# Three chained layers on one core: weight tiles shared by two batches, an attention with more buffers, another place for the decoding

## The chip, the cores and the metric

The kernel runs on one core of one Trainium2 chip. The metric is the device time of one execution in microseconds (us). The kernel before takes 1176.02 us, the median of three runs (1173.72 to 1176.10).

## The reference

Three layers follow each other, for 4 batches (B) of 448 positions (S) and 768 features (12 heads of 64):

```python
scores = scale * np.matmul(q, k.transpose(0, 1, 3, 2))      # causal mask, softmax over the last axis
x = softmax(scores) @ v                                     # B, S, 768
h = x.transpose(0, 2, 1) @ U @ V                            # low rank: 448 -> 32 -> 448 along S
u = x + h.transpose(0, 2, 1)
x = u + np.maximum(u @ w_ch1, 0.0) @ w_ch2                  # 768 -> 3072 -> 768
logits = x @ w_gate                                         # 4 experts, the best 2 of each position
out = sum(w[e] * (softmax_causal(x @ wq[e], x @ wk[e]) @ (x @ wv[e])) @ wo[e] for e in chosen)
```

Inputs and weights arrive as 64-bit floats.

## The kernel before, in words

**Numbers.** Matrix products run in float16 with each operand cut into a high and a low half, and three of the four products of halves are added (`PASS`), so that a product of a 128x128 weight block with 448 columns is three matmuls of 128x448. The 64-bit weights are *decoded* on the core: VectorE makes a float32 from the two words (`decode`, one TENSOR_SCALAR and two SCALAR_TENSOR_TENSOR of 128x768), ScalarE squares it for a norm, TensorE adds the norm up over the partitions (a 128x1 matmul), ScalarE scales and casts the high half, GpSimd subtracts it for the low half. `weight_tile` does this for one of 48 tiles of the MLP (the 768-3072-768 layer), stores the result to HBM (`W16`), and on a later use loads the tile from there in place of decoding it. The raw tile lands in one of two buffers (`RAW`).

**Stages.** The MLP has 4 groups of 12 tiles: 6 tiles of the first matrix and 6 of the second. A *product* is what one tile does for one batch: 18 matmuls of 128x448. `mlp(g, b)` is group g for batch b: 6 products into the hidden buffer `HID` (one buffer), 6 products added to the batch's float32 state `X3`. So a batch has 48 products, the kernel 192. `attention(b)` is the first layer of batch b with the low-rank step behind it, as 6 *pairs* of heads, counted through: batch 0 has pairs 0 to 5, batch 1 pairs 6 to 11, and so on. For each pair `softmax` makes scores on TensorE, masks and scales them on VectorE, takes exponentials on ScalarE (four per head, 112x112 to 112x448), casts the high halves of P by `HIGH` (two of four on ScalarE, two on VectorE), subtracts on GpSimd for the low halves, and transposes both by DMA; `weighted` multiplies with V, `lowrank` does the step behind. `split_u` then cuts the batch's u into halves for the MLP, which can not start before. `experts(b)` is the last layer of batch b.

**Order.** The program is recorded first, in the order of the string `ORDER`: attention of batch 0 (a0), of batch 1 (a1), MLP of batch 0 (m00 to m03), experts of batch 0 (e0), a2, the MLP of batch 1, e1, a3, the MLP of batch 2, e2, the MLP of batch 3, e3. Then `Program.issue` plans it: it walks all five engines with costs per instruction (`cost`), and of what is ready takes the smallest key. Attention has keys that rise by 4500 per half pair (`HT`), MLP products have a large one (`FILL`), so they fill what is left; decoding has the keys of `first_key`. The result is one fixed order of instructions for each engine, and on the chip each engine runs its own in order. Where the plan has TensorE idle before `WARM_END`, it puts in dummy matmuls (line 953). All planned instructions are issued at line 250, so the rows below are told apart by shape.

**Memory.** Weight tiles live in a ring of `NW` = 19 slots. `SLOTS` gives batch 0's attention more buffers for P than the others (5 instead of 3, and 4 instead of 2 for its halves), since the buffers of batch 1 are idle then. `BANKS` says which of 8 PSUM banks a stage uses; MLP products of batch 0 use two of them ("f").

Of the kernel before, what the change touches and what calls it, by code (L numbers as in the profile page):

```python
# [21 lines left out]
C = 112  # L22
NC = S // C
KD = D // 128
NG = 4
# [5 lines left out]
HIGH = ("act", "act", "dve", "dve")  # L31
# [11 lines left out]
WARM_START, WARM_END, WARM_GAP = 3000.0, 130000.0, 100.0  # L43
NW = 19
# [3 lines left out]
ORDER = "a0 a1 m00 m01 m02 m03 e0 a2 m10 m11 m12 m13 e1 a3 m20 m21 m22 m23 e2 m30 m31 m32 m33 e3"  # L48
# [4 lines left out]
class Program:  # L53
# [7 lines left out]
    def __init__(self):  # L61
        self.ops = []
        self.key = 0.0
        self.group_op = None
        self.state = {}
        self.near = {}
        self.pitch = {}
        self.idle = None

# [54 lines left out]
    def cost(self, name, method, outs, ins, kw):  # L124
        o = outs[0]
        n = 1
        for c in o.shape[1:]:
            n *= c
        if name == "pe":
            f = 4.0 if ins[0].dtype == F32 else 1.0  # L130
            c = f * max(n / 2.4 + 2.5, 36.0)
            self.work = c * (ins[0].shape[0] / 128.0) * (o.shape[0] / 128.0)

            return c * (0.62 if HD in (o.shape[0], ins[0].shape[0]) and n >= C else 1.0)
        ptr = sum(x.free_size() == 1 and n > 1 for x in ins)
        psum = any(a.space == bass.MemoryType.PSUM for a in outs + ins)
        if name == "act" and method == "dma_start":
            return 300.0
        if name == "act":
            src = 51.0 if ins[0].space == bass.MemoryType.PSUM else 94.0  # L140
            return src + n / 1.2 + 93.0 * (ptr + len(outs) - 1)
        if name == "dve":
            m = 1
            for c in ins[0].shape[1:] if ins else o.shape[1:]:
                m *= c
            m = max(m, n)
            fast = not psum and method in ("tensor_scalar", "tensor_copy", "memset")
            two = not psum and n > 32 and (fast or sum(x.free_size() > 1 for x in ins) > 1)
            return ((64.0 + (m / 2 if fast else m)) / 0.96 + 64.0 * ptr) * (1.2 if two else 1.0)
        if name == "pool":  # L150
            if method == "partition_all_reduce":
                return 374.0
            return 148.0 + 1.89 * n if method == "tensor_tensor" else 260.0 + 2.5 * n
        return 350.0 + outs[0].nbytes() / 292.0 if method == "dma_start_transpose" else 650.0

    def add(self, name, method, fn, a, k):
        outs, ins = [], []
        for key, x in list(enumerate(a)) + list(k.items()):
            if hasattr(x, "ap"):
                (outs if key in (0, "out", "accum_out") else ins).append(x)  # L160
        self.work = 0.0
        cost = self.cost(name, method, outs, ins, k)
        data = 0.0
        if method.startswith("dma"):
            nbytes = max(x.nbytes() for x in outs + ins)
            data = nbytes / (185.0 if method == "dma_start_transpose" else 360.0)
        deps = set()
        i = len(self.ops)
        if self.group_op:
            i -= 1  # L170
        for x in ins:
            r = self.region(x)
            if r is not None:
                for q in self.touching(r):
                    deps.update(self.state[q][0])
                self.state[r][1].append(i)
        for x in outs:
            r = self.region(x)
            if r is not None:
                for q in self.touching(r):  # L180
                    w, rd = self.state[q]
                    deps.update(w)
                    deps.update(rd)
                    if q[1] >= r[1] and q[2] <= r[2] and q[3] >= r[3] and q[4] <= r[4]:
                        w[:] = [i]
                        rd[:] = []
        deps.discard(i)
        if self.group_op:
            op = self.ops[-1]
            op["calls"].append((fn, a, k))  # L190
            op["cost"] += cost
            op["work"] += self.work
            op["deps"] |= deps
        else:
            op = dict(eng=name, cost=cost, data=data, deps=deps, calls=[(fn, a, k)], key=self.key,
                      work=self.work)
            self.ops.append(op)
            if self.group_op is False:
                self.group_op = True

    def issue(self):
# [9 lines left out]
        bus = 0.0  # L211
# [7 lines left out]
        while done < len(ops):  # L219
# [33 lines left out]
            if n == "pe":  # L253
# [4 lines left out]
                if not warm:  # L258
                    cost *= 2.0
            end = t + cost  # L260
# [15 lines left out]
def kernel(  # L276
# [44 lines left out]
    BANKS = {"s": (0, 1), "o": (2,), "l": (3, 4), "m": (5, 6, 7), "f": (5, 6), "r": (7,), "x": (5, 6), "y": (2, 7), "b": (3, 4)}  # L321
# [16 lines left out]
    HID = view("hid", 0, 128, F16, GF * 2 * S).rearrange("p (f l s) -> p f l s", f=GF, l=2)  # L338
# [10 lines left out]
    def hslot(r, o):  # L349
        return view(r, o, C, F16, 2 * NBLK * 128)  # L350

    SLOTS = [
        (P32[0:3] + [pslot("x3", 10752), pslot("x3", 10752 + 4480)], PHL[0:2] + [hslot("uh", 5376), hslot("ul", 5376)]),
        (P32[0:3], PHL[0:2]), (P32[0:3], PHL[0:2]), (P32[0:3], PHL[0:2]),
# [130 lines left out]
    def softmax(terms, nes, pts, last=False, kind="s", first=False):  # L485

        ps, hs = P32[0:3], PHL[0:2]
        if last:
            ps, hs = P32, PHL
        elif first:  # L490
            ps, hs = SLOTS[0]
# [28 lines left out]
        for j in range(2):  # L520
# [14 lines left out]
            sp.dma_start_transpose(out=PT[pts[j]], in_=h16[j])  # L535
# [26 lines left out]
    def weighted(vs, pts, y, dst, coef=None, kind="o"):  # L562
        shares(y, coef)
        t = psum(kind)
        with prog.group():
            for i, (lp, lv_) in enumerate(PASS):
                for j in range(NC):
                    for h, (va, pt) in enumerate(zip(vs, pts)):
# [4 lines left out]
                           PT[pt][0:C, k:k + kc * (NC - 1 - j) + 1:kc],  # L573
# [37 lines left out]
    def attention(b):  # L611
# [6 lines left out]
        for p in range(NP):  # L618
# [6 lines left out]
            if p == NP - 1 and b + 1 < B:  # L625
                v_scale(b + 1)
            i = n % 2
            prog.key = HT * 2 * n
            softmax([[(QK[i][64 * j:64 * j + 64, 1], QK[i][64 * j:64 * j + 64, 0])] for j in range(2)], -0.125,
                    [(2 * n + j) % 3 for j in range(2)], first=b == 0)  # L630
            prog.key = HT * (2 * n + 1)
            weighted([VH[:, 2 * i + j] for j in range(2)], [(2 * n + j) % 3 for j in range(2)], X3[b][:, p], XHL[i])
# [19 lines left out]
    kept = [False]  # L652
# [78 lines left out]
    def mlp(g, b):  # L731
        if b == 0:
            factors(g)
        ut = (UH[b], UL[b])
        for f in range(GF):
            early = g + b + f == 0
            t = psum("m" if kept[0] else "f")
            wt = [a.rearrange("p (k m) -> p k m", k=KD) for a in tiles[2 * GF * g + f]]
            prog.key = FILL - early
            product(t[:, 0:S], [(wt[lw][:, k], ut[lx][:, k]) for k in range(KD) for lw, lx in PASS])  # L740
            prog.key = URGENT
            act.activation(t[:, 0:S], t[:, 0:S], AF.Relu, scale=(RF if b else RF0)[:, g * GF + f:g * GF + f + 1])
            act.activation(HID[:, f, 0], t[:, 0:S], AF.Copy)
            dve.tensor_tensor(out=HID[:, f, 1], in0=t[:, 0:S], in1=HID[:, f, 0], op=ALU.subtract)
        cf, ct = CF[g % 2], CTS[g % 2]
        dve.tensor_scalar(ct, PRS[:, g:g + 1], 2.0 ** 54 / HCAP, PU[:, b:b + 1], op0=ALU.mult, op1=ALU.mult)
        dve.tensor_scalar(cf, PW2[:, g * GF:g * GF + KD], 2.0 ** 83, ct, op0=ALU.mult, op1=ALU.mult)
        for d in range(KD):
            t = psum("m" if kept[0] else "f")
            wt = [a.rearrange("p (k m) -> p k m", k=GF) for a in tiles[2 * GF * g + GF + d]]  # L750
            prog.key = FILL
            product(t[:, 0:S], [(wt[lw][:, f], HID[:, f, lx]) for f in range(GF) for lw, lx in PASS])
            prog.key = URGENT
            dve.scalar_tensor_tensor(out=X3[b][:, d], in0=t[:, 0:S], scalar=cf[:, d:d + 1], in1=X3[b][:, d],
                                     op0=ALU.mult, op1=ALU.add)
            if g == NG - 1:
                absmax(AMX[:, b * KD + d:b * KD + d + 1], X3[b][:, d])

    def experts(b):
# [3 lines left out]
        free = 3072 * next(i for i in range(NW - 5) if not held & set(range(i, i + 6)))  # L763
        if last:
            qo, vo, yo, xo = ("hid", 0), ("ring", free), ("hid", 7168), ("ring", free + 4096)
# [6 lines left out]
        if last:  # L772
            OST = [view("ring", free + 6144 + i * 1792, 128, F32, S) for i in range(6)]
        else:
            OST = [view("rd", 14848 + i * 1792, 128, F32, S) for i in range(2)]
        pts = (0, 1, 2, 3) if last else (0, 1, 0, 1)
# [126 lines left out]
    zero_pads(SLOTS[0][1])  # L903
# [25 lines left out]
    def first_key(i):  # L929
        return HT * (1 + 0.9 * i if i < 2 * GF else 12 + (i - 2 * GF) / 3)  # L930

    def group(b, g):
        for i in range(2 * GF * g, 2 * GF * (g + 1)):
            prog.key = URGENT if b else first_key(i)
            weight_tile(i, not b)
        mlp(g, b)
# [13 lines left out]
    for step in ORDER.split():  # L950
        kind, b = step[0], [int(c) for c in step[1:]]
        {"a": attention, "m": group, "e": moe}[kind](*b)
# [47 lines left out]
```

## Time and profile before

| | |
|---|---|
| median of three runs | 1176.02 us |
| the profiled execution | 1177.93 us |
| its span, first to last instruction | 1176.2 us |
| TensorE busy | 1088.9 us (93%), 392 dummy matmuls in it |
| VectorE busy | 678.1 us (58%) |
| ScalarE busy | 546.7 us (46%) |
| GpSimd busy | 371.3 us (32%) |
| DMA | 162 loads and 54 stores of 384 KB tiles, 48 of 768 KB raw tiles, 88 transposes |
| granted TensorE clock, mean | 0.967 of full speed |

A share over the whole span says little here, since the stages have different limits. The profile is read by stretches: 0 to 150 us (attention of batch 0, with decoding), 150 to 391.4 us (attention of batch 1, the rest of the decoding, MLP of batch 0), 391.4 to 975 us (MLP of batches 1 and 2, attention of batches 2 and 3, experts of batches 0 and 1), 975 to the end (the rest of batch 3).

### The profile page before, as it was taken

How to read it: one execution, taken by the hardware profiler on the slowest of the kernel's cores; microseconds unless marked ns; L12 is line 12 of the kernel's file. 1: busy time of each engine (PE TensorE's matmuls, PEld its weight loads, DVE VectorE, ACT ScalarE, POOL GpSimd, SP SyncE). 2: the span in 40 equal slices, each digit the busy share in tenths (PEclk: the TensorE clock that was granted, in tenths of full speed). 3: DMA queues.
4: the chain of work that ended last, by engine and by line, in shares of the span. 5: the costliest groups of instructions: out<-in, count | busy, mean ns of one | idle time of the engine just before them, and what ended most of it. 6: DMA issues, size and time to landing. Idle time of an engine off the chain costs nothing.

```text
span 1176.2 us, 18782 instructions
## 1 busy us (share of the span) xinstructions
PE 1088.9 (93%) x6888; PEld 571.7 (49%) x6888; DVE 678.1 (58%) x1831; ACT 546.7 (46%) x1317; POOL 371.3 (32%) x419
## 2 busy tenths in 40 slices
PE   7899969979988999999999999999999997899895
PEld 3454434434444455445555554455555544355452
DVE  8869888998889765665432555654224333111453
ACT  4755767676577544575412456652122323121142
POOL 3755755766453102454200034540000012000012
PEclk9999978998999999999999999999999998999998
DMA  7887888897786754998734349984443255331023
GB/s 195 208 195 245 211 199 242 260 229 206 230 265 222 239 189 112 213 231 200 175 108 120 96 107 216 234 180 118 122 121 108 82 131 112 125 121 54 1 40 87
DMA packets 220141, 192.57 MB, mean 164 GB/s; under 512 B 176304, under 2 KB 179504, under 8 KB 220048
## 3 DMA queue, kind: packets, MB, share of 16 engines
q1 hardware_dynamic: 220048, 191.36, 61.0%
q8 instruction: 54, 0.88, 0.3%
q14 instruction: 39, 0.32, 0.1%
HBM read 121.60 MB, written 26.74 MB: 126 GB/s over the span
## 4 chain that ended last, share of the span: by engine, by line
PE 65%; DVE 9%; issue 3%; ACT 3%; DMA 2%; POOL 2%; POOLq 0%; SPq 0%; DVEq 0%; ACTq 0%
PE bank L250 65%; DVE arena L250 9%; ACT arena L250 2%; POOL arena L250 2%; DMA arena<-in_v_dram 1%; DMA arena<-in_w_dram 0%; DMA arena<-in_we_dram 0%; DMA arena<-w 0%; ACT bank L250 0%; POOLq L995 0%; SPq L250 0%; DVEq L250 0%; ACTq L250 0%; POOLq L250 0%
## 5 line engine op out<-in xcount | busy, mean ns | idle before, releaser
L250 PE MATMUL bank<-arena 128*128 128x448 f16 (+12 forms) x6496 | 1006.5, 332 | 70.0 <-DVE arena L250 40.8
L250 PEld LDWEIGHTS <-arena 128*128 128x128 f16 (+4 forms) x5960 | 489.2, 106 | 489.8 <-issue 124.9
L250 POOL TENSOR_TENSOR arena<-arena 112x336 f16<-112x336 f32 (+6 forms) x408 | 369.1, 924 | 796.2 <-ACT arena L250 719.6
L250 ACT ACTIVATE arena<-arena 128x768 f16<-128x768 f32 (+10 forms) x671 | 376.6, 591 | 282.8 <-DVE arena L250 267.6
L250 DVE TENSOR_TENSOR arena<-bank,arena 128x448 f16<-128x448 f32 (+2 forms) x160 | 95.4, 600 | 215.2 <-ACT arena L250 183.4
L250 DVE CUSTOM_DVE_ANT_0 arena<-bank,arena 112x112 f32<-112x112 f32 (+4 forms) x280 | 125.7, 475 | 62.6 <-PE bank L250 55.1
L250 ACT ACTIVATE bank<-bank,arena 128x448 f32<-128x448 f32 x96 | 57.8, 603 | 222.8 <-PE bank L250 221.8
L250 DVE SCALAR_TENSOR_TENSOR arena<-bank,arena 128x448 f32<-128x448 f32 (+1 forms) x120 | 73.4, 614 | 148.0 <-PE bank L250 125.0
L250 DVE SCALAR_TENSOR_TENSOR arena<-arena 128x768 int32<-128x768 int32 (+5 forms) x159 | 154.9, 993 | 5.3 <-ACT arena L250 4.2
L250 ACT ACTIVATE arena<-bank 128x448 f16<-128x448 f32 (+2 forms) x160 | 82.6, 523 | 74.7 <-PE bank L250 72.8
L250 DVE TENSOR_SCALAR arena<-arena 128x1 f32<-128x1 f32 (+9 forms) x367 | 90.7, 267 | 20.1 <-ACT arena L250 9.7
L953 PE MATMUL bank<-arena 128*128 128x448 f16 x392 | 89.8, 376 | 13.4 <-DVE arena L250 12.4
L250 DVE CAST arena<-arena 112x336 f16<-112x336 f32 (+2 forms) x160 | 85.4, 547 | 2.1 <-PE bank L250 1.0
L250 PEld LDWEIGHTS bank<-arena 64*112 64x112 f32 (+5 forms) x536 | 49.4, 176 | 55.9 <-issue 18.9
L953 PEld LDWEIGHTS <-arena 128*128 128x128 f16 x392 | 39.1, 105 | 54.3 <-issue 25.9
L250 DVE TENSOR_REDUCE arena<-arena 128x1 f32<-128x448 f32 (+7 forms) x107 | 58.2, 546 | 9.5 <-DMA arena<-in_v_dram 5.2
L250 ACT ACTIVATION_READ_ACCUMULATOR arena<-arena 112x1 f32 (+1 forms) x304 | 57.0, 188 | 0.0
L250 ACT ACTIVATE arena<-bank,arena 64x128 f16<-64x128 f32 (+3 forms) x85 | 34.2, 405 | 44.6 <-PE bank L250 38.7
L250 DVE TENSOR_TENSOR arena<-arena 112x8 f16<-112x8 f32 (+4 forms) x69 | 24.6, 368 | 1.4
L250 DVE DVE_READ_ACCUMULATOR2_ANT arena<- 112x1 f32 (+1 forms) x280 | 22.7, 81 | 0.0
L250 DVE TENSOR_SCALAR arena<-bank 128x1 f32<-128x1 f32 x48 | 7.2, 149 | 12.8 <-PE bank L250 12.7
L250 DVE RECIPROCAL arena<-arena 112x8 f32<-112x8 f32 (+1 forms) x36 | 7.0, 195 | 0.7
(12 smaller groups left out, 13.6 us busy)
## 6 DMA issues: line engine op xcount, KB each, us to landing
arena<-w SPq DMA_DIRECT2D x162, 384.0 KB, 3.3
arena<-in_w_dram SPq DMA_DIRECT2D x48, 768.0 KB, 5.6
w<-arena SPq DMA_DIRECT2D x54, 384.0 KB, 3.1
arena<-in_qk_dram SPq DMA_DIRECT2D x24, 448.0 KB, 5.6
arena<-in_v_dram SPq DMA_DIRECT2D x24, 224.0 KB, 5.0
out_dram<-arena SPq DMA_DIRECT2D x24, 224.0 KB, 2.6
arena<-in_we_dram SPq DMA_DIRECT2D x6, 384.0 KB, 4.6
arena<-arena SPq DMA_TRANSPOSE x88, 4.6
```

Of the source, the lines that this page charges most:

```text
L250: fn(*a, **k)
L953: prog.idle = lambda: nc.tensor.matmul(bank[:, 7, 64:512], ZERO.to_broadcast([128, 128]), ZERO.to_broadcast([128, S]), start=True, stop=True)
```

## The change

- `ORDER` becomes "a0 a1 m00 m01 m101 m20 m30 e0 a2 m21 m31 e1 a3 m02 m12 m22 m32 e2 m03 m13 m23 m33 e3". The first digit is now the group, the rest are the batches: m101 is group 1 for batches 0 and 1. Both attentions come first, then group 0 for batch 0 and for batch 1 with the same 12 tiles, group 1 for both in turn, tile by tile, then groups 2 and 3 for batch 0, its experts, and so on. `group` loads or decodes tiles only where the group differs from the last one; 24 of the 144 reloads go.
- `first_key` moves the decoding back: the 12 tiles of group 0 are spread over both attentions, the other 36 have keys behind them.
- `HIGH`: all high halves of P on ScalarE.
- `SLOTS`: the second attention has 5 and 4 buffers too.
- The hidden buffer is doubled, and the ring has 15 slots for it. MLP products use four PSUM banks ("g") between the second attention and the first expert stage.
- The planner's costs: VectorE and GpSimd instructions that use the port they share are planned one after the other, transposes are planned as faster, dummies go on to 210000 of the planner's units.

```diff
-HIGH = ("act", "act", "dve", "dve")
+HIGH = ("act", "act", "act", "act")
...
-WARM_START, WARM_END, WARM_GAP = 3000.0, 130000.0, 100.0
-NW = 19
+WARM_START, WARM_END, WARM_GAP = 3000.0, 210000.0, 100.0
+NW = 15
...
-            two = not psum and n > 32 and (fast or sum(x.free_size() > 1 for x in ins) > 1)
-            return ((64.0 + (m / 2 if fast else m)) / 0.96 + 64.0 * ptr) * (1.2 if two else 1.0)
+            self.port = not psum and n > 1 and (fast or sum(x.free_size() > 1 for x in ins) > 1)
+            return (64.0 + (m / 2 if fast else m)) / 0.96 + 64.0 * ptr + 80.0 * (self.port and n > 32)
...
+            if o["port"]:
+                t = max(t, port)
+                port = t + cost
...
-        ("ring", NW * 3072), ("rd", RD), ("hid", GF * 2 * S * 2),
+        ("ring", NW * 3072), ("rd", RD), ("hid", 2 * GF * 2 * S * 2),
...
+    SPARE = [hslot("uh", 5376), hslot("ul", 5376)]
     SLOTS = [
-        (P32[0:3] + [pslot("x3", 10752), pslot("x3", 10752 + 4480)], PHL[0:2] + [hslot("uh", 5376), hslot("ul", 5376)]),
-        (P32[0:3], PHL[0:2]), (P32[0:3], PHL[0:2]), (P32[0:3], PHL[0:2]),
+        (P32[0:3] + [pslot("x3", 10752), pslot("x3", 10752 + 4480)], PHL[0:2] + SPARE, PT[0:3]),
+        (P32[0:3] + [pslot("hid", 10752), pslot("hid", 10752 + 4480)], PHL[0:2] + SPARE, PT[0:3]),
+        (P32[0:3], PHL[0:2], PT[0:3]), (P32[0:3], PHL[0:2], PT[0:3]),
     ]
...
-    def mlp(g, b):
-        if b == 0:
+    def mlp(g, bs):
+        if 0 in bs:
             factors(g)
-        ut = (UH[b], UL[b])
+        bank = "m" if kept[0] else "g" if started[0] else "f"
         for f in range(GF):
...
+            for b in bs:
+                early = g + b + f == 0
+                t = psum(bank)
+                wt = [a.rearrange("p (k m) -> p k m", k=KD) for a in tiles[2 * GF * g + f]]
...
     def first_key(i):
-        return HT * (1 + 0.9 * i if i < 2 * GF else 12 + (i - 2 * GF) / 3)
+        return HT * (1 + 2.6 * i if i < 2 * GF else 32 + (i - 2 * GF) / 3)
...
+    def group(g, bs):
+        if last_group[0] != g:
+            for i in range(2 * GF * g, 2 * GF * (g + 1)):
+                prog.key = URGENT if g in made else first_key(i)
+                weight_tile(i, g not in made)
+            made.add(g)
+            last_group[0] = g
+        mlp(g, bs)
```

How the change moves instructions, at two places. The first is VectorE at the decoding of tile 27 (of 48). Before, this stands in the middle of pair 10's softmax: 128x768 are the decoding, "ISA" rows of 112 partitions the masking of scores, 128x448 evictions of MLP products, 128x1 the small steps of a norm.

```order
L250 TENSOR_SCALAR arena<-arena 128x768
L250 SCALAR_TENSOR_TENSOR arena<-arena 128x768
L250 TENSOR_SCALAR arena<-bank 128x1
L250 ISA arena<-bank,arena 112x448
L250 ISA arena 112x1
L250 TENSOR_SCALAR arena<-arena 128x1
L250 SCALAR_TENSOR_TENSOR arena<-arena 128x768
L250 TENSOR_SCALAR arena<-arena 128x1
L250 ISA arena<-bank,arena 112x448
L250 ISA arena 112x1
L250 TENSOR_TENSOR arena<-bank,arena 128x448
L250 TENSOR_SCALAR arena<-arena 128x1
```

In the changed kernel the same decoding stands in the MLP of group 1:

```order
L252 TENSOR_SCALAR arena<-arena 128x768
L252 TENSOR_SCALAR arena<-bank 128x1
L252 TENSOR_TENSOR arena<-bank,arena 128x448
L252 TENSOR_SCALAR arena<-arena 128x1
L252 SCALAR_TENSOR_TENSOR arena<-arena 128x768
L252 TENSOR_SCALAR arena<-arena 128x1
L252 SCALAR_TENSOR_TENSOR arena<-arena 128x768
L252 TENSOR_SCALAR arena<-arena 128x1
L252 TENSOR_TENSOR arena<-bank,arena 128x448
```

No softmax stands there any more: for one decoded tile there are two evictions, one of each batch. On TensorE the norms of tiles 0 to 9 stand before the last scores of the second attention and those of tiles 10 to 14 before the first product of batch 1; before, all 48 stand ahead of batch 1's first.

The second place is the SP queue, which issues all DMAs, at the load of pair 4's q and k (in_qk). Before, it stands behind the transposes (128x20x112) of pair 3:

```order
L250 DMA_TRANSPOSE arena<-arena 128x20x112
L250 DMA_TRANSPOSE arena<-arena 128x8x128
L250 DMA_TRANSPOSE arena<-arena 128x20x112
L250 DMA arena<-in_v_dram 112x512
L250 DMA arena<-in_w_dram 128x768 x2
L250 DMA arena<-in_qk_dram 128x896
L250 DMA arena<-in_v_dram 112x512
```

In the changed kernel it stands between the two transposes of pair 1:

```order
L252 DMA_TRANSPOSE arena<-arena 128x20x112
L252 DMA_TRANSPOSE arena<-arena 128x8x128
L252 DMA arena<-in_qk_dram 128x896
L252 DMA arena<-in_w_dram 128x768
L252 DMA_TRANSPOSE arena<-arena 128x20x112
L252 DMA w<-arena 128x1536
L252 DMA arena<-in_v_dram 112x512
```

The loads of a pair have moved ahead by two pairs of transposes.

## Rows read from the trace of the kernel before

**Rows 1.** Busy time: stretch, us, PE, PEld, DVE, ACT, POOL (instructions), PEclk, DMA share, GB/s

```profile
0.00:150.00 150.00, 131.35 (x854) 66.09 (x855) 125.04 (x369) 93.50 (x239) 91.44 (x102) 0.96 0.79 208
150.00:391.40 241.40, 202.88 (x1242) 105.66 (x1242) 210.71 (x504) 165.62 (x335) 130.70 (x124) 0.92 0.83 235
391.40:975.00 583.60, 582.32 (x3806) 308.98 (x3807) 281.76 (x812) 241.19 (x633) 128.32 (x167) 1.00 0.59 153
975.00:1176.20 201.20, 172.33 (x988) 90.99 (x988) 60.60 (x148) 46.38 (x112) 20.80 (x27) 0.92 0.28 75
```

**Rows 2.** The same of line 953 (dummy matmuls) alone: PE, PEld

```profile
0.00:150.00 150.00, 87.19 (x386) 38.34 (x387) 0.96 0.79 208
150.00:391.40 241.40, 2.60 (x6) 0.73 (x5) 0.92 0.83 235
```

**Rows 3.** Chain that ended last: start us, us, what

```profile
391.40 159.20 PE bank L250 x1096
...
983.64 10.51 issue
...
1003.09 4.17 DMA arena<-w
```

**Rows 4.** Groups by shape, TensorE, to 391.4 us, then from there: busy, mean ns

```profile
L250 PE MATMUL bank<-arena 128*128 128x448 f16 x756 | 161.8, 364 | 18.3 <-DVE arena L250 16.4 <-ACT arena L250 1.6
...
L250 PE MATMUL bank<-arena 128*128 128x448 f16 x3132 | 623.0, 356 | 12.0 <-DVE arena L250 3.9 <-DMA arena<-w 3.0 <-ACT arena L250 2.8
```

**Rows 5.** Busy time, 1025 to 1050 us

```profile
1025.00:1050.00 25.00, 25.00 (x134) 12.92 (x132) 3.91 (x7) 5.44 (x10) 0.00 (x0) 1.00 0.40 124
```

**Rows 6.** Groups by shape, ScalarE, 7.5 to 126.6 us

```profile
L250 ACT ACTIVATE arena<-arena 128x768 f16<-128x768 f32 x21 | 18.5, 880 | 13.1 <-DVE arena L250 12.9
L250 ACT ACTIVATE arena<-arena 112x448 f32<-112x448 f32 x12 | 7.9, 657 | 0.0
```

**Rows 7.** The same, 470 to 559 us

```profile
L250 ACT ACTIVATE arena<-arena 112x448 f32<-112x448 f32 x12 | 7.9, 659 | 2.3 <-DVE arena L250 2.3
```

**Rows 8.** Busy time, 470 to 559 us

```profile
470.00:559.00 89.00, 88.93 (x662) 44.90 (x661) 54.80 (x183) 53.67 (x161) 43.61 (x58) 1.00 0.91 215
```

**Rows 9.** Timeline of ScalarE: start us, us, instruction

```profile
590.51 2.89 ACT L250 ACTIVATE arena<-arena 128x448 f16<-128x448 f32 x5
```

**Rows 10.** Groups by shape, whole span: busy us, mean ns, idle before

```profile
L250 DVE SCALAR_TENSOR_TENSOR arena<-arena 128x768 int32<-128x768 int32 x96 | 109.2, 1139 | 0.6
L250 DVE TENSOR_TENSOR arena<-bank,arena 128x448 f16<-128x448 f32 x112 | 69.0, 621 | 165.0 <-ACT arena L250 164.4
L250 DVE CAST arena<-arena 112x448 f16<-112x448 f32 x64 | 42.4, 663 | 0.5 <-ACT arena L250 0.5
L250 DVE TENSOR_SCALAR arena<-arena 128x768 int32<-128x768 int32 x48 | 35.0, 730 | 7.4 <-DMA arena<-in_w_dram 3.7 <-POOL arena L250 3.2 <-issue 0.2
L250 DVE CAST arena<-arena 112x336 f16<-112x336 f32 x64 | 31.7, 506 | 0.1
L250 ACT ACTIVATE arena<-arena 112x224 f16<-112x224 f32 x64 | 23.5, 376 | 0.2
```

**Rows 11.** Timeline of VectorE, then of GpSimd

```profile
51.46 2.06 DVE L250 CAST arena<-arena 112x336 f16<-112x336 f32 x1
...
49.84 4.92 POOL L250 TENSOR_TENSOR arena<-arena 112x224 f16<-112x224 f32 x4
```

**Rows 12.** Timeline of the SP queue (DMA issues), 73 to 85 us

```profile
73.39 9.72 SPq L250 DMA_TRANSPOSE arena<-arena  x3
...
84.97 0.43 SPq L250 DMA_DIRECT2D arena<-in_qk_dram  x1
```

**Rows 13.** SP queue, raw weight loads of tiles 34 and 47

```profile
301.80 0.37 SPq L250 DMA_DIRECT2D arena<-in_w_dram  x1
...
372.00 0.33 SPq L250 DMA_DIRECT2D arena<-in_w_dram  x1
```

**Rows 14.** Groups by shape, TensorE, 423 to 593.4 us

```profile
L250 PE MATMUL bank<-arena 128*128 128x448 f16 x612 | 124.5, 353 | 0.0
```

More of the change, by code (lines that the diff above doesn't have):

```diff
@@ L483, in scaled_copy, with softmax @@
             dve.tensor_scalar(o, a, scale, None, op0=ALU.mult)
-    def softmax(terms, nes, pts, last=False, kind="s", first=False):
+    def softmax(terms, nes, pts, last=False, kind="s", slots=None):
         ps, hs = P32[0:3], PHL[0:2]
@@ L489, in softmax @@
             ps, hs = P32, PHL
-        elif first:
-            ps, hs = SLOTS[0]
+        elif slots:
+            ps, hs = slots
         k = heads[0]
@@ L762, in experts @@
         held = {(ring_n[0] - 1 - i) % NW for i in range(NE)}
-        free = 3072 * next(i for i in range(NW - 5) if not held & set(range(i, i + 6)))
+        two = 3072 * next(i for i in range(NW - 1) if not held & {i, i + 1})
         if last:
-            qo, vo, yo, xo = ("hid", 0), ("ring", free), ("hid", 7168), ("ring", free + 4096)
+            qo, vo, yo, xo = ("hid", 0), ("ring", two), ("hid", 7168), ("ring", two + 4096)
         else:
@@ L772, in experts @@
         if last:
-            OST = [view("ring", free + 6144 + i * 1792, 128, F32, S) for i in range(6)]
+            OST = [view("hid", 10752 + i * 1792, 128, F32, S) for i in range(6)]
         else:
             OST = [view("rd", 14848 + i * 1792, 128, F32, S) for i in range(2)]
-        pts = (0, 1, 2, 3) if last else (0, 1, 0, 1)
+        pts = PT if last else PT[0:2] * 2
         ks, ko, kl = "xyy" if last else "sll" if b == B - 2 else "sol"
@@ L929, in first_key @@
     def first_key(i):
-        return HT * (1 + 0.9 * i if i < 2 * GF else 12 + (i - 2 * GF) / 3)
[L932 to L936, printed above, removed]
+        return HT * (1 + 2.6 * i if i < 2 * GF else 32 + (i - 2 * GF) / 3)
+    made = set()
+    last_group = [None]
+    def group(g, bs):
[6 more added lines that the diff above has]
+        mlp(g, bs)
     def moe(b):
@@ L950 @@
     for step in ORDER.split():
-        kind, b = step[0], [int(c) for c in step[1:]]
-        {"a": attention, "m": group, "e": moe}[kind](*b)
+        kind, bs = step[0], [int(c) for c in step[1:]]
+        if kind == "a":
+            attention(*bs)
+            started[0] = bs[0] == 1
+        elif kind == "e":
+            moe(*bs)
+            last_group[0] = None
+        else:
+            group(bs[0], bs[1:])
     prog.idle = lambda: nc.tensor.matmul(bank[:, 7, 64:512], ZERO.to_broadcast([128, 128]), ZERO.to_broadcast([128, S]), start=True, stop=True)
```

77 lines of the change are left out of this document (42 added, 35 removed).

## The prediction

> **What bounds the kernel now.** I read the busy time by stretch first [rows 1], then the chain that ended last [rows 3], then the groups by shape. From 391.4 to 975 us TensorE is busy 582.3 of 583.6 us at full clock: here only matmuls count. Ahead of that it isn't TensorE: up to 391.4 us it is busy 334.2 us, and 89.8 of these are dummies [rows 2]. VectorE is busy 125.0 of the first 150 us and 210.7 of the next 241.4, the fullest engine of both. So the kernel has two parts, one that VectorE and the waits around it set, and one that TensorE sets. The chain says the same: from 391.4 us it runs on TensorE for 159 us at a stretch, and leaves it for long only near 983 and 1003 us [rows 3].
>
> How much is done in the first part? The 128x448 matmuls are 756 up to 391.4 us [rows 4], or 42 products of 18: batch 0's MLP but for its last six. Behind stand 3132: 150 products (2700) and 432 of the four expert stages. At peak 134 of them take 25.0 us [rows 5], 0.1866 us each, 3.36 us a product.
>
> **The change, as a sum.** I call S the time at which batch 1's first product starts in the changed kernel. By the order of instructions only batch 0's group 0 (12 products) is done by then, so 180 products are left where at 391.4 us 150 were left. The rest is the same work. So the span is S + (1176.2 - 391.4) + 30 x 3.36 = S + 784.8 + 100.7 = S + 885.5, plus what the new second part loses. Below S = 290.7 the change gains.
>
> *S.* In the first attention, 7.5 to 126.6 us holds 12 exponentials of 112x448, two a pair, so 6 pairs at 19.85 us each; 21 casts or squares of 128x768, two a tile, say that 10.5 tiles were decoded there, 1.75 a pair [rows 6]. The third attention has no decoding beside it: 89 us for 6 pairs, 14.8 each [rows 7]. The difference, 5.0 us, is 2.9 us a decoded tile. The changed order has 10 norms ahead of the second attention's last scores, 0.83 a pair: 14.8 + 0.83 x 2.9 = 17.2 us. Before, the second attention has its 6 pairs among 30 tiles and three MLP groups; that falls away. Its larger buffers and the earlier loads are in this pace: in the SP queue three transposes held it from 73.4 to 83.1 us, and pair 4's loads came only at 84.97 [rows 12]; they now stand ahead of these.
>
> *The casts.* Per pair, two of 112x336 (0.506 us) and two of 112x448 (0.663) leave VectorE, 2.34 us [rows 10]. ScalarE gets four; it shows none of these shapes. From below they cost 0.376 us (its cast of 112x224, rows 10), from above 0.657 (its 112x448 exponential, rows 6): 1.5 to 2.6 us a pair, I take 2.1. So a pair's pace moves by something between -2.3 and +2.6 us; I take -1.2, half of what VectorE gives up, since the trace has VectorE as the fuller engine. Pace 16.0, bounds 14.9 and 19.8. A cast of 112x336 that began at 51.46 us took 2.06 us while GpSimd ran four subtractions without a pause from 49.84 to 54.76 us [rows 11]: four times its mean.
>
> The Trainium skill (SBUF — State Buffer, Who interferes with whom) says that a VectorE cast in a two-port mode and a GpSimd instruction lock each other out for a whole instruction. The row agrees; by that rule alone the casts give back their full 2.34 us and GpSimd's waits too, and the sum would be some 14 us lower.
>
> Behind the third attention's last softmax, at 559 us, come 34.4 us of weighting, low rank and splitting until its u is cut, at 593.4 us [rows 9]. S = 7.5 + 12 x 16.0 + 34.4 = 233.9. A bound from VectorE's load: 335.8 us busy up to 391.4 [rows 1], less 30 tiles of 0.730 + 2 x 1.139 = 3.0 us (90.2), less 48 casts (28.1), leaves 217.4; at the first stretch's density (125.0 of 150) that is 261 us, not counting the evictions and small steps that go too. From below: pairs at 14.8 - 2.3 = 12.5 us give 192.
>
> *The second part.* Two terms. (a) 33 tiles are now decoded between S and the norm of tile 47, and the norms stand in TensorE's stream among products it could do: 879 of the 128x448, 164.0 us, 4.97 us a tile. Before, with little else in the way, the raw loads of tiles 34 and 47 are 70.2 us apart [rows 13], 5.40 us a tile, which is 14.2 us more in all. From above: a tile now has nearly two products' evictions beside it, not one, 0.62 us more on VectorE [rows 10]: 6.02 us, 34.7 in all. From below 0, where the loads have the queue to themselves. I take 7. (b) Beside the first expert stage and the third attention, 423 to 593.4 us, TensorE did 612 of the 128x448, 108 of them the experts' own, so 504 of products [rows 14]; in the changed order 393 stand there, since batch 1 has only two groups left. If those stages need their 170 us anyway, TensorE idles 111 x 0.1866 = 20.7 us; if not, nothing. VectorE is busy 54.8 of 89 us there and ScalarE 53.7, so there is room [rows 8], though DMA's share is 0.91. I take 5.
>
> *At nothing.* The 24 reloads saved: the DMA share in the MLP is 0.40 [rows 5], so they are hidden, and were. Four fewer ring slots: in a run of products a slot's tile comes free 14 products, 47 us, before its next is wanted. Dummies: they fill idle time. The last expert attention has no cover: its two pairs' casts change it by -5 to +5 us, taken at 0. Stalls near 983 and 1003 us [rows 3], transposes and then a weight load behind them, stay: the order there has the same pieces.
>
> The Trainium skill (Perfetto Trace Analysis, Optimizing Scalar/DVE Operations) holds that an operation with a fast mode is quicker on VectorE, and that moving it pays where VectorE is saturated. It isn't from 470 us on [rows 8], so by that rule the later pairs lose a little; here a cast's mean on VectorE, 0.51 to 0.66 us, is no shorter than my estimate for ScalarE, so I add nothing. By the rule the sum would be up to 4 us higher.
>
> **Sum.** 233.9 + 885.5 + 7 + 5 = 1131.4 us of span. The profiled execution took 1.7 us more than its span and 1.9 more than the median, so span and median differ by 0.2 us: 1131.
>
> **Rivals.**
> - *Decoding sets the pace of the MLP behind it.* TensorE waits at norms, 6.02 us a tile: 1131.4 - 7 + 34.7 = 1159 us. For it: 5.40 us a tile was reached with one batch's evictions. Against: no softmax shares VectorE there now.
> - *Too little to do beside the third attention.* 1131.4 - 5 + 20.7 = 1147 us. For it: DMA at 0.91. Against: TensorE never waited there, so nothing shows that the stages need the 170 us.
> - *ScalarE becomes the engine that each pair waits for (slower than before).* It has exponentials, casts, V and decoding, and if a pair keeps the first attention's 19.85 us and the casts come on top, the pace is 21.95 us, S = 7.5 + 263.4 + 34.4 = 305.3, the span 1203 us. It decides from a pace of 19.7 us on. For it: 19.85 is what the first attention did with these buffers. Against: ScalarE was busy 93.5 of 150 us there, and decoding per pair halves.
>
> That the sharing does nothing is part of the forecast: what gains is the place of the work, not the saved loads.
>
> **Chances.** Forecast 0.56; decoding 0.19; cover 0.17; ScalarE 0.08. The likeliest's own range, with pace 14.9 to 17.5, is 1118 to 1150. For 8 in 10 I go to 1105 below (a pace of 14.9 with nothing lost behind gives 1106) and to 1165 above, past both rivals that still gain. A measurement can't tell a change under 0.2%. Faster 0.91, same 0.02, slower 0.07: only the last rival, and not all of it, ends above 1178.
>
> **What would show it.** Right: batch 1's first product near 234 us, the 12 pairs 16 us apart, then TensorE busy to near 930 us with no dummies. S wrong: ScalarE over nine tenths busy up to S, or long gaps before scores. (a) wrong: TensorE waiting for ScalarE or VectorE at 128x1 matmuls between 234 and 410 us. (b) wrong: gaps of TensorE before the cut of batch 2's u. Wrong as a whole: a pace over 19.7 us a pair, or a second part in which TensorE is under 95% busy.

## The result and the profile after

The changed kernel takes 1123.1 us (median of 4 runs, 1116.7 to 1124.5) against 1176.1: ratio 0.954, interval 0.950 to 0.958. The prediction was 1131 with a range of 1105 to 1165. The profiled execution's span is 1122.8 us.

Busy time by stretch, changed kernel: stretch, us, PE, PEld, DVE, ACT, POOL (instructions), PEclk, DMA share, GB/s.

```profile
0.00:222.30 222.30, 211.30 (x1550) 110.05 (x1551) 177.39 (x542) 175.55 (x456) 135.23 (x162) 1.00 0.87 217
222.30:434.60 212.30, 210.94 (x1155) 113.07 (x1153) 158.90 (x338) 124.81 (x200) 77.29 (x68) 1.00 0.65 216
434.60:770.00 335.40, 323.84 (x2348) 173.39 (x2347) 167.36 (x566) 201.57 (x568) 117.18 (x154) 0.99 0.69 162
770.00:952.00 182.00, 172.48 (x1004) 91.84 (x1003) 52.66 (x132) 52.17 (x119) 13.20 (x18) 0.99 0.40 116
952.00:1122.80 170.80, 152.83 (x883) 82.31 (x880) 52.15 (x127) 41.84 (x102) 13.28 (x18) 0.95 0.27 77
```

The boundary between the two parts, at 391.4 us in [rows 1], is now at 222.3 us: S, the start of batch 1's first product. In the row that ends there three resources are busy at once, and none is full: VectorE 80%, ScalarE 79%, DMA 0.87. TensorE's 211.3 us are again filled with dummies, as in [rows 2]; here are theirs alone (PE, PEld):

```profile
0.00:222.30 222.30, 96.12 (x436) 40.90 (x436) 1.00 0.87 217
```

From S on TensorE idles 1.4 + 11.6 + 9.5 + 18.0 = 40.4 us; from 391.4 us on it idled 30.2 before. Its busy time from S is 860.1 us; before it was 754.7 from 391.4, and the 30 products that move over make that 855.4. So the second part is 900.5 us: the 885.5 of the prediction, 10.2 more idle and 4.7 more busy.

The chain that ended last, changed kernel: start us, us, what.

```profile
529.04 8.21 DMA arena<-arena
...
759.83 138.68 PE bank L252 x774
...
920.64 11.07 issue
...
938.73 3.01 DMA arena<-w
```

The two late stalls of [rows 3] are both still there, as predicted. New are the transposes (a DMA from arena to arena) between 460 and 750 us, with short pieces of ScalarE and GpSimd between them; before, the chain ran on TensorE there but for some 9 us near 700.

### The profile page after: what moved, and what is told of

It is laid out like the page before. It is cut to its first block, busy times and chain, and to the rows that moved or that the text cites. A ratio compares the mean times of both kernels' runs of the same rounds, so it can differ in the third digit from the quotient of the medians.

```text
span 1122.8 us, 18857 instructions
## 1 busy us (share of the span) xinstructions
PE 1071.4 (95%) x6932; PEld 570.7 (51%) x6932; DVE 608.5 (54%) x1703; ACT 595.9 (53%) x1445; POOL 356.2 (32%) x419
## 4 chain that ended last, share of the span: by engine, by line
PE 41%; DMA 8%; ACT 4%; issue 3%; POOL 2%; DVE 1%; SPq 1%; POOLq 0%; ACTq 0%; DVEq 0%
PE bank L252 41%; DMA arena<-arena 6%; ACT arena L252 3%; POOL arena L252 2%; DVE arena L252 1%; DMA out_dram<-arena 1%; SPq L252 1%; DMA arena<-w 1%; DMA arena<-in_v_dram 0%; ACT bank L252 0%; POOLq L1029 0%; POOLq L252 0%; ACTq L252 0%; DVEq L252 0%
## 5 line engine op out<-in xcount | busy, mean ns | idle before, releaser
L252 PE MATMUL bank<-arena 128*128 128x448 f16 (+11 forms) x6496 | 985.7, 327 | 45.5 <-DMA arena<-arena 18.3
L252 POOL TENSOR_TENSOR arena<-arena 128x384 f16<-128x384 f32 (+6 forms) x408 | 354.0, 889 | 757.6 <-ACT arena L252 732.4
L252 ACT ACTIVATE arena<-arena 112x112 f32<-112x112 f32 (+13 forms) x799 | 431.9, 578 | 209.8 <-DVE arena L252 169.8
L252 DVE SCALAR_TENSOR_TENSOR arena<-arena 128x768 int32<-128x768 int32 (+6 forms) x159 | 150.7, 968 | 2.1 <-ACT arena L252 1.3
L252 DVE TENSOR_SCALAR arena<-arena 128x1 int32<-128x1 int32 (+8 forms) x367 | 84.9, 254 | 36.8 <-ACT arena L252 21.7
L987 PE MATMUL bank<-arena 128*128 128x448 f16 x436 | 96.1, 362 | 2.0 <-DVE arena L918 1.0
L252 DVE TENSOR_REDUCE arena<-arena 128x1 f32<-128x448 f32 (+6 forms) x107 | 57.8, 545 | 4.6 <-DMA arena<-in_we_dram 2.3
L252 ACT ACTIVATE arena<-bank,arena 64x128 f16<-64x128 f32 (+2 forms) x85 | 34.1, 406 | 39.2 <-PE bank L252 32.7
L252 DVE CAST arena<-arena 112x8 f16<-112x8 f32 x32 | 15.5, 486 | 3.7 <-PE bank L252 3.4
L252 DVE TENSOR_REDUCE arena<-bank 1x1 f32<-1x128 f32 (+2 forms) x14 | 3.9, 276 | 7.9 <-PE bank L252 7.9
```

The source lines that it names most:

```text
L252: fn(*a, **k)
L987: prog.idle = lambda: nc.tensor.matmul(bank[:, 7, 64:512], ZERO.to_broadcast([128, 128]), ZERO.to_broadcast([128, S]), start=True, stop=True)
```

## The experiments

"Time" is the median; the ratio is to the kernel before, with its interval; the changed kernel has 0.954. Runs of one kernel lie up to 9 us apart, so single profiles differ by some us without a reason. Differences are those of the medians; the kernel before took 1172.9 to 1176.1 us beside the several runs, so by the ratios they come out up to 5 us larger.

**Only the order and its due times undone.**

```
-ORDER = "a0 a1 m00 m01 m101 m20 m30 e0 a2 ..."   # groups for two batches
+ORDER = "a0 a1 m00 m10 m20 m30 e0 a2 m01 m11 ..."
-  1 + 2.6 * i if i < 2 * GF else 32 + (i - 2 * GF) / 3
+  1 + 0.9 * i if i < 2 * GF else 12 + (i - 2 * GF) / 3
```

(and the dummies' end in the plan at 130 us, as before)

> The changed kernel with the old order and decoding keys alone: group by group for one batch (group 0 to 3 of batch 0, then e0, a2, batch 1), decoding among both attentions, dummies to 130000. Theory (the place of the decoding and of the products makes the gain): batch 1's first product comes no sooner than 360 us, dummy-free TensorE from about 390 us, and the time goes back to 1160 to 1178 us. Rival (the attention itself became faster by casts, buffers and planning; the order is only along): the first part shortens anyway and the time stays under 1140 us.

1185.4 us, ratio 1.009 (1.007 to 1.012). That is 7 us above the theory's range, and the rival (under 1140) is excluded. The casts, the buffers and the planner's costs without the order make the kernel slower: 62 us lie between the two orders, and nothing of the gain is left in the old one. The order, the due times of the decoding and the sharing of tiles, which the old order has no place for, were undone together; only the sharing has runs of its own, further below.

```profile
0.00:270.50 270.50, 231.32 (x1566) 123.21 (x1567) 197.09 (x598) 197.46 (x488) 157.70 (x177) 0.92 0.83 209
270.50:406.50 136.00, 125.34 (x670) 66.39 (x668) 111.11 (x236) 86.69 (x137) 61.48 (x52) 0.96 0.74 247
```

Busy time as above, this kernel. The second attention ends at 270 us instead of 221, since more tiles are decoded beside it, and TensorE waits 10.7 us in the next 136. Batch 1's first relu comes at 406.5 us, so its first product starts near 403.

**The same and the casts back on VectorE.**

```
-HIGH = ("act", "act", "act", "act")
+HIGH = ("act", "act", "dve", "dve")
```

> Old order and keys and casts as before; the rest (buffers, 15 slots, two hidden buffers, four PSUM banks, planner's costs) as changed. Theory: the casts gain only where the attentions stand alone in front; with decoding among them VectorE is full of it and ScalarE too, so against e5 (1185 us) the time changes by under 8 us: 1177 to 1190 us, no faster than the kernel before. Rival A (casts on ScalarE hurt where decoding is among the attentions): 1165 to 1174 us. Rival B (the casts help everywhere by 2 us a pair): 1205 us or more.

1207.8 us, ratio 1.030 (1.028 to 1.033): the theory fell and rival B holds, the casts bring 22 us in the old order too. What is left of the change (ring of 15 slots, two hidden buffers, the planner's costs, borrowed buffers), put into the old order, costs 32 us against the kernel before. I did not take this apart further.

**Only the casts back**, by the same line, in the new order.

> The changed kernel with two of four casts back on VectorE. Theory: the first part grows by 0.5 to 1.2 us a pair (6 to 14 us), and of the 11.4 us in which TensorE idles beside the third and fourth attention most goes, since the casts on ScalarE lengthen each pair there: 1118 to 1130 us, batch 1's first product at 228 to 236 us. Rival A (the casts make the gain): over 1140 us. Rival B (the idle time there comes from transposes planned as faster, not from the casts): the idle time stays at 8 us or more, and the time is 1129 to 1137 us.

1155.0 us, ratio 0.983 (0.980 to 0.986): rival A. 32 us are lost, 27 of them before S. ScalarE's timeline shows where: the first exponential, the last pair's first one of 112x448 and batch 1's first relu in this kernel, then the last two in the changed one, whose first exponential is at 17.68.

```profile
17.79 0.39 ACT L252 ACTIVATE arena<-arena 112x112 f32<-112x112 f32 x1 [15.71 <-DVE arena L252]
...
203.27 0.67 ACT L252 ACTIVATE arena<-arena 112x448 f32<-112x448 f32 x1 [1.08 <-DVE arena L252]
...
252.83 1.18 ACT L252 ACTIVATE bank<-bank,arena 128x448 f32<-128x448 f32 x2 [0.94 <-PE bank L252]
```

```profile
176.01 0.67 ACT L252 ACTIVATE arena<-arena 112x448 f32<-112x448 f32 x1 [0.50 <-DVE arena L252]
...
225.75 0.61 ACT L252 ACTIVATE bank<-bank,arena 128x448 f32<-128x448 f32 x1 [4.25 <-PE bank L252]
```

By their first exponentials the pairs start 16.0 us apart, with the change 13.7; 27 us over 12 pairs are 2.25 us a pair. VectorE is as full as in the changed kernel, 196.25 of the first 248 us (79%). The casts by shape up to 222.3 us, busy and mean ns, first this kernel, then the changed one:

```profile
L252 DVE CAST arena<-arena 112x448 f16<-112x448 f32 x24 | 18.4, 787 | 0.0
L252 DVE CAST arena<-arena 112x336 f16<-112x336 f32 x24 | 15.1, 650 | 0.1
```

```profile
L252 ACT ACTIVATE arena<-arena 112x448 f16<-112x448 f32 x24 | 13.3, 562 | 0.0
L252 ACT ACTIVATE arena<-arena 112x336 f16<-112x336 f32 x24 | 11.3, 471 | 0.0
```

By the means they take 2.87 us a pair on VectorE here, not the 2.34 of [rows 10], and 2.07 us on ScalarE (2.1 was estimated). The row's mean runs over the whole span, and a cast is longer beside GpSimd's work. The same cast beside three subtractions, GpSimd's row for them, and the cast alone:

```profile
141.55 2.16 DVE L252 CAST arena<-arena 112x336 f16<-112x336 f32 x1
...
141.21 3.17 POOL L252 TENSOR_TENSOR arena<-arena 112x512 f16<-112x512 f32 x3 [1.23 <-ACT arena L252]
...
187.32 0.32 DVE L252 CAST arena<-arena 112x336 f16<-112x336 f32 x1
```

Of the 24 casts of 112x336 up to 222.3 us, the 12 that share less than 0.1 us with a GpSimd instruction took 0.33 us each and the other 12 took 0.97 in the mean; of 112x448, 3 took 0.38 alone and 21 took 0.85 beside GpSimd. So alone a cast was quicker on VectorE than on ScalarE, and about half of the 2.87 us is lengthening.

**Casts on ScalarE only in the first two attentions** (k counts heads as they are recorded, two a pair).

```
+HIGH2 = ("act", "act", "dve", "dve")
...
-  scaled_copy(HIGH[c], ...
+  scaled_copy((HIGH if k < 24 else HIGH2)[c], ...
```

> The changed kernel with all casts on ScalarE only in the first two attentions; behind them two of four are back on VectorE. With all of them back (e1) the first part grew by 27 us. Theory: the 27 us came from the first two attentions alone, so batch 1's first product stays at 220 to 230 us, and behind it the stretch from the first expert stage to the cut of batch 3's u shrinks from 331 to about 323 us as in e1: 1110 to 1122 us. Rival (the gaps beside the third and fourth attention are the luck of a plan): no shorter than now, 1120 to 1132 us.

1125.0 us, ratio 0.959 (0.956 to 0.962): no difference that can be told from the changed kernel, so the rival's range and not the theory's. In the profile the stretch that the theory names is 321.6 us, as it said, but what follows is 8 us longer; and the run with the old buffers below has 321.0 with all casts on ScalarE. All of the casts' gain lies ahead of S; behind it VectorE isn't what is waited for.

**The second attention with the old buffers.**

```
-  (P32[0:3] + [pslot("hid", 10752), pslot("hid", 10752 + 4480)], PHL[0:2] + SPARE, PT[0:3]),
+  (P32[0:3], PHL[0:2], PT[0:3]),
```

> The changed kernel with 3 and 2 buffers for P in the second attention as before. Theory: the pace of its six pairs is set by VectorE and ScalarE, so buffers are worth little: pairs 6 to 11 slow by 0 to 1.5 us each, 1123 to 1132 us. Rival (buffers set the pace of a pair): 2.5 us or more a pair, over 1138 us.

1120.8 us, ratio 0.954 (0.951 to 0.957). That is 2 us under the theory's range: the borrowed buffers are worth nothing. S is 4 us later in the profile and the rest earlier.

**The planner's old costs**: no lock between VectorE and GpSimd, old times of both, and the transposes'.

```
-  self.port = True
-  return 150.0 + 2.0 * n if method == "tensor_tensor" else 260.0 + 2.5 * n
+  return 148.0 + 1.89 * n if method == "tensor_tensor" else 260.0 + 2.5 * n
...
-  self.port = not psum and n > 1 and ...
-  return (64.0 + (m / 2 if fast else m)) / 0.96 + 64.0 * ptr + 80.0 * (self.port and n > 32)
+  two = not psum and n > 32 and ...
+  return ((64.0 + (m / 2 if fast else m)) / 0.96 + 64.0 * ptr) * (1.2 if two else 1.0)
...
-  data = nbytes / (292.0 if method == "dma_start_transpose" else 360.0)
+  data = nbytes / (185.0 if method == "dma_start_transpose" else 360.0)
```

> The changed kernel planned with the old costs: no shared port in the plan, transposes at 185 in place of 292 bytes per ns. Theory: the first part gets gaps again, since VectorE and GpSimd wait for each other unplanned (S 5 to 15 us later), but beside the third and fourth attention TensorE's idle 11.4 us falls under 4 since slower planned transposes leave room: 1118 to 1132 us. Rival (casts on ScalarE make those gaps): the idle time stays at 8 us or more and the time is 1128 to 1140 us.

1141.4 us, ratio 0.971 (0.967 to 0.975), 1 us above the rival's range: the new costs are worth 18 us. S is 5 us later in its profile, as the theory had it; the gaps beside the later attentions don't shrink, and the rest of the 18 is spread over what follows. Beside the third attention alone TensorE waits 14.7 us at a clock of 0.93 (4.7 with the new costs); some of that comes back beside the fourth (0.9 us there, 6.9 with the new costs):

```profile
447.70:623.70 176.00, 161.25 (x1153) 86.01 (x1152) 89.91 (x298) 105.22 (x291) 59.63 (x78) 0.93 0.67 158
```

**Of these the transposes' cost alone** (the last two lines of that diff).

> The changed kernel with transposes planned at 185 bytes per ns as before, the shared port still planned. All old costs together lost 18 us (e3). Theory: that loss is the unplanned port, so with the port planned and only transposes slower the first part keeps within 5 us (batch 1's first product at 220 to 232 us) and the gaps beside the third and fourth attention shrink: 1115 to 1128 us. Rival (the transposes' cost makes the loss): 1135 us or more.

1126.7 us, ratio 0.961 (0.958 to 0.963): 3 to 4 us of the 18, little more than the spread, so the rest comes from the costs of VectorE and GpSimd and their lock in the plan. In the profile S is 7 us later, and 9.3 us of gaps stay beside the two later attentions.

**No sharing.** Groups 0 and 1 are loaded again for batch 1, group 1 is done for each batch by itself.

```
-ORDER = "a0 a1 m00 m01 m101 m20 ..."
+ORDER = "a0 a1 m00 m01 m10 m11 m20 ..."
-  if last_group[0] != g:
+  if g not in made or last_group[0] != (g, bs):
...
-  last_group[0] = g
+  last_group[0] = (g, bs)
```

> The changed kernel without shared tiles: batch 1 loads group 0 and group 1 again (24 loads of 384 KB more), and group 1 is done for batch 0 and then for batch 1. Theory: the loads are hidden, so the time stays within 6 us of the changed kernel (1117 to 1129 us). Rival (sharing is what lets decoding keep up: with group 1 taken for one batch at a time, TensorE meets tiles not yet decoded): TensorE idles between 222 and 435 us by 10 us or more, 1133 us or more.

1149.3 us, ratio 0.981 (0.978 to 0.984): 26 us lost. The prediction had the saved loads at nothing. The rival has the time right and the reason wrong: TensorE is busy from 246 to 440 us without a gap, and S itself is 20 us later. So most of the loss lies ahead of S, where I had not looked for reloads. The next two runs take its halves.

**Only group 0 loaded again.**

```
-  if last_group[0] != g:
+  if last_group[0] != g or (g, bs) == (0, [1]):
```

> The changed kernel (1123.1 us), but batch 1 loads the 12 tiles of group 0 again; the pairing of batches 0 and 1 in group 1 stays. Without any sharing it took 1149.3 us, and 12 reloads (4.7 MB in all) stand in SP's queue among the loads, transposes and stores of the first two attentions, up to 246 us. Theory A, these early reloads cost: batch 1's first product goes from 222 to about 243 us, the DMA share up to there from 0.88 to above 0.91, the time is 1140 to 1150 us. Rival B, the pairing of two batches in group 1 is what gains: S stays at 222 us, the time 1121 to 1127 us.

1139.1 us, ratio 0.968 (0.965 to 0.972): 16 us, 1 below the bound of theory A, and S is 21 us later.

**Only group 1 loaded again**, and done for each batch by itself.

```
-ORDER = "a0 a1 m00 m01 m101 m20 ..."
+ORDER = "a0 a1 m00 m01 m10 m11 m20 ..."
-  if last_group[0] != g:
+  if last_group[0] != g or (g, bs) == (1, [1]):
```

> The changed kernel (1123.1 us), but group 1 is done for batch 0 and then for batch 1, with its 12 tiles loaded again; group 0 is loaded once for both. Most of these reloads stand behind batch 1's first product, beside 212 us in which TensorE hardly waits. Theory A (reloads cost only where they stand in front of the attentions' transfers): 1121 to 1130 us, first product of batch 1 at 222 to 228 us. Rival B (sharing a tile between two batches is itself the gain, since a tile is then decoded every 6.7 us and not every 3.4): TensorE waits for norms of group 1 and the time is 1138 to 1150 us.

1123.4 us, ratio 0.956 (0.954 to 0.958): nothing lost. Theory A holds: the pairing of two batches doesn't gain, and reloads behind S are free; the 12 that go out ahead of S cost. Busy time up to 222.3 us, reloading group 0, then group 1:

```profile
0.00:222.30 222.30, 200.53 (x1475) 103.95 (x1475) 164.69 (x515) 166.42 (x444) 135.94 (x159) 0.99 0.96 229
```

```profile
0.00:222.30 222.30, 211.21 (x1548) 109.79 (x1549) 177.87 (x542) 175.57 (x456) 134.38 (x162) 0.99 0.88 217
```

The DMA share goes from 0.88 to 0.96, and VectorE and ScalarE do less in the same time. The SP queue's own waits in that stretch (us in total, times, longest us) and the issues of the reloads (count, KB each, median us to landing), group 0 loaded again:

```profile
SPq L252 <- DMA w<-arena: 17.5, 5, 6.1
```

```profile
arena<-w SPq DMA_DIRECT2D x12, 384.0 KB, 3.9
```

A reload reads what the store of the decoded tile wrote. SP waits for that store at 5 of them, 17.5 us in all, and the attentions' loads and transposes stand behind it in the same queue. The changed kernel shows no such wait; but all of SP's waits up to there are 150 us with the reloads and 158 without, so the 17.5 aren't simply added. The other transfers take longer too, the transposes for one (median us to landing, reloading group 0, then group 1):

```profile
arena<-arena SPq DMA_TRANSPOSE x35, 5.5
```

```profile
arena<-arena SPq DMA_TRANSPOSE x36, 4.6
```

The pairs keep their pace: the second attention's last exponential ends at 178.3 us, at 177.3 in the changed kernel. The 21 us come behind it. The chain of the run that reloads group 0 goes through transfers there, and the attention's last transpose is issued at 222.4 us, not at 200.7:

```profile
180.50 10.02 DMA arena<-arena
...
205.98 7.93 DMA arena<-in_w_dram
...
222.36 5.32 DMA arena<-arena
```

Whether the 4.7 MB or the wait for the stores makes the 21 us wasn't separated; nor why no sharing loses 10 us more than its two halves.

**Batch 1's group 1 behind the first expert stage**, to have more work beside the third and fourth attentions.

```
-ORDER = "a0 a1 m00 m01 m101 m20 m30 e0 a2 m21 ..."
+ORDER = "a0 a1 m00 m01 m10 m20 m30 e0 a2 m11 m21 ..."
```

> The changed kernel (1123.1 us), but batch 1's group 1 (12 products, 40.3 us) stands behind the first expert stage instead of beside batch 0's, so that it is there to be done beside the third and fourth attentions; its tiles are loaded again. Theory C, TensorE idles 11.6 us between 435 and 770 us because too little is left to do there: these gaps fall to under 3 us, and decoding 33 tiles in 172 us instead of 212 costs less than that, 1112 to 1120 us. Rival D, with 5.2 us a tile left the decoding sets the pace (5.4 us a tile was the fastest before): TensorE waits 7 us or more between 222 and 400 us, the time is 1121 to 1135 us. Rival E, the gaps beside these attentions come from the order of the transfers and not from lack of work: they stay at about 10 us, 1123 us.

1139.2 us, ratio 0.969 (0.966 to 0.972), slower than any of the three expected; its profiled execution (1134.1) is the fastest of its four. D's waits and E's gaps both appear there, C's gain doesn't. Decoding: TensorE waits 9.7 us of the 195.7 from S to the expert stage; the norm matmuls between 340 and 400 us show it (busy, mean ns, idle before):

```profile
L252 PE MATMUL bank<-arena 128*128 128x1 f32 x20 | 3.4, 239 | 5.1 <-ACT arena L252 5.1
```

Cover: the gaps stay, 6.8 and 5.2 us in the two attentions' stretches, while 42 us between them are plain products without any gap:

```profile
418.00:571.50 153.50, 146.66 (x1107) 79.38 (x1105) 80.19 (x275) 98.05 (x280) 59.62 (x78) 1.00 0.74 180
571.50:613.50 42.00, 42.00 (x224) 21.50 (x222) 14.19 (x28) 6.76 (x12) 0.00 (x0) 1.00 0.39 116
613.50:766.90 153.40, 148.25 (x1104) 80.18 (x1103) 76.51 (x264) 98.02 (x279) 57.37 (x76) 0.99 0.71 161
```

There was work, but the plan had put it elsewhere: into those 42 us. Beside the two attentions stand 485 and 486 matmuls of 128x448, fewer than the changed kernel's 516 and 566. So the run does not test what more work at the gaps would do.

**Dummies only up to 130 us of the plan**, as before: 344 instead of 436.

```
-WARM_START, WARM_END, WARM_GAP = 3000.0, 210000.0, 100.0
+WARM_START, WARM_END, WARM_GAP = 3000.0, 130000.0, 100.0
```

> The changed kernel (1123.1 us), but the dummy matmuls end in the plan at 130 us as before, not at 210: 344 of them instead of 436. Theory A (prediction: they fill idle time and cost or bring nothing): granted clock lower between 130 and 222 us, but first product of batch 1 at 219 to 227 us and 1120 to 1128 us in all. Rival B: at the lower clock the second attention's matmuls get longer and delay each of its pairs; first product at 232 us or later, time 1131 to 1145 us.

1125.8 us, ratio 0.960 (0.955 to 0.965), S 4 us later: theory A. Busy time, this kernel, then the changed one:

```profile
130.00:222.30 92.30, 77.81 (x539) 42.18 (x538) 76.77 (x204) 69.32 (x167) 54.34 (x59) 0.85 0.92 228
```

```profile
130.00:222.30 92.30, 89.18 (x664) 47.53 (x663) 79.43 (x207) 74.84 (x177) 52.68 (x60) 1.00 0.86 216
```

The granted clock, a mean over the stretch, is 0.85 instead of 1.00 there, and the end is the same within the spread of the runs.

None of the twelve beats the changed kernel by more than that spread.

## Why the prediction held, and where its terms were off

**What bounds the kernel: right.** The kernel has the two parts, the first ends earlier, the second costs what the products cost. The old order puts batch 1's first product near 403 us, and with it all the gain is gone. TensorE is busy 95.5% of the second part, just above the 95% that the prediction set as its bound.

**S: 12 us too late, with a pace that was further off.** Predicted 7.5 + 12 x 16.0 + 34.4 = 233.9. Measured: first exponential at 17.7, 12 pairs of 13.8 to 183.6, u cut at 220.7 (37.1 behind the last softmax), first product at 222.3. The pace takes off 26 us and lies under its stated bound of 14.9; the later start, the longer tail and the step to the first product put some 14 back on, and the second part 3 more than was summed. So that the time came within 9 us of the sum is in part luck.

```profile
17.68 0.39 ACT L252 ACTIVATE arena<-arena 112x112 f32<-112x112 f32 x1 [15.60 <-DVE arena L252]
```

That is ScalarE's first exponential in the timeline: it waits 15.6 us for VectorE. With the planner's old costs it comes at 8 us, and S is no earlier; a later start is not a later S, and start and pace can't be taken one by one.

The pace is the mis-sized term. With the casts still on VectorE the kernel has 16.0, where the sum had 17.2. The 1.2 lies in the price of decoding or in the 14.8 under it, and no run says in which: 14.8 is the third attention's 89 us over 6 pairs and holds the end of the last one, while the first exponentials of these pairs are 13.2 us apart (470.0 to 536.2 us). The casts' 1.2 was half of the 2.25 they give. I took half of what VectorE gives up, at a price from the whole span; each pair got 2.25 of 2.87 us, with ScalarE at 79%.

The Trainium skill (SBUF — State Buffer, Who interferes with whom) has a VectorE cast in a two-port mode and a GpSimd instruction lock each other out. The trace agrees on the cast's side: up to 222.3 us none of the 15 casts that GpSimd shares less than 0.1 us with took 0.40 us, and others took up to 2.16; what the lock costs GpSimd wasn't measured. By this rule the casts were to give back their full price, and the sum was 14 us lower. I showed the rule with a row and then took the other value.

**(a) Decoding behind S: right in size, wrong in kind.** I priced 7 us of waiting. TensorE waits 1.4 us in the 212. What it pays is its own work, by shape from 222.3 to 434.6 us (busy, mean ns):

```profile
L252 PE MATMUL bank<-arena 128*128 128x448 f16 x1085 | 210.4, 352 | 0.0
L252 PE MATMUL bank<-arena 128*128 128x1 f32 x66 | 9.7, 216 | 0.7 <-ACT arena L252 0.7
```

66 small norm matmuls, 9.7 us, moved from a part where TensorE idled into one where it sets the time. The sum had no term for them. Waiting appears (9.7 us) when 33 tiles have 196 us and not 212, as the run with group 1 later shows. Net busy time rose by only 4.7; I read the rest as given back at the end, where the clock is 0.95 from 952 us on and was 0.92 from 975 [rows 1], but no run isolates it.

**(b) Beside the later attentions: 11.6 us, 5 predicted.** Beside the third, which the term was for, it is 4.7; 6.9 are beside the fourth, which I had not looked at. The wait, by shape from 434.6 to 770 us:

```profile
L252 PE MATMUL bank<-arena 112*64 112x448 f16 x96 | 22.4, 362 | 6.7 <-DMA arena<-arena 6.7
```

These are the products of P with V, waiting for P's transposes; one takes 4 to 8 us in the chain. The reason in the prediction, too little to do, stays open: with 12 more products to do the gaps stay, but the plan put these elsewhere. The gaps also stay with two of four casts back on VectorE there (9.7 us) and with the transposes' old cost (9.3).

**At nothing.** Borrowed buffers, the 92 added dummies and the later pairs' casts: right, each by its run. The four ring slots have no run of their own. The saved reloads: wrong, 26 us when neither group is shared. I took the DMA share of a run of products, 0.40 [rows 5], but the 12 reloads of group 0 go out ahead of S, where [rows 1] has 0.79 and 0.83. Since the changed kernel doesn't make them, the sum came out without this term; the sentence that the sharing does nothing fell. The planner's costs had no price at all and are worth 18 us.

**Rivals.** ScalarE as the engine that each pair waits for: excluded, pace 13.7. Decoding sets the pace: not here, but with 16 us less room TensorE waited 9.7 us. The cover beside the third attention: 4.7 of its 20.7 us appeared, its reason is open.

The Trainium skill (Perfetto Trace Analysis, Optimizing Scalar/DVE Operations) says that such a move may make sense where VectorE is saturated; the runs agree: with VectorE busy 79% it gave 27 us ahead of S, and nothing that can be measured behind it.

## What to carry over

Price a move between engines with durations of its own stage: a mean over the span hid nearly a fifth of what the casts cost beside GpSimd (2.34 of 2.87 us). Ask of a saved transfer not whether transfers are hidden on average but where its issue stands in the queue and what stands behind it: 12 reloads cost 16 us among the attentions' transfers and 12 others nothing behind them. When work moves from a part where TensorE idles into one that it sets, its own small matmuls count too.

## What the runs showed of the hardware

- A cast of 112x336 took 0.33 us on VectorE with under 0.1 us of a GpSimd instruction beside it, 0.97 in the mean and up to 2.16 with more, and 0.47 on ScalarE; one of 112x448 took 0.38, 0.85 and 0.56 (up to 222.3 us, casts back and changed kernel).
- Loads that read back what a store had just written held the SP queue up to 6.1 us each, 17.5 us at 5 of them.
- A granted clock of 0.85 in place of 1.00 over 92 us, with TensorE busy 77.8 us there and not 89.2, moved the end by nothing that the runs can tell.
